# An arena of 29 score slots, divided triples, and an output stage in phases of eight scores

## The chip, the cores and the metric

The kernel runs on one core of a Trainium2 chip, in fp32 throughout (matmuls in fp32 and in the fp32r form). The metric is the device time of one execution in microseconds, the median of the runs shown. Five engines work side by side, each through its own list of instructions in program order: TensorE (PE) multiplies, VectorE (DVE) and ScalarE (ACT) work elementwise, GpSimd (POOL) does small jobs here, and SyncE (SP) issues nearly all DMAs. Semaphores order them against each other. SBUF holds the tiles; PSUM has eight banks that take TensorE's results.

## What is computed

Two blocks read the same x of 2048 rows and 512 columns, and a gate of each row mixes them:

```python
def _A_ref(x, wqkv, wo):
    H = 32; Dh = D // H
    q, k, v = ...                                  # x @ wqkv, 32 heads of 16
    scores = jnp.einsum("bhqd,bhkd->bhqk", q, k) * Dh ** -0.5
    p = _softmax(scores, axis=-1)
    o = jnp.einsum("bhqk,bhkd->bhqd", p, v)
    return o.transpose(0, 2, 1, 3).reshape(B, S, D) @ wo

def _B_ref(x, w1, b1, w2, b2):                     # across the 2048 rows
    h = _layernorm(x, axis=-1)
    u = _gelu(jnp.einsum("bsd,sf->bdf", h, w1) + b1)
    y = jnp.einsum("bdf,fs->bds", u, w2) + b2
    return y.transpose(0, 2, 1)

g = _sigmoid((x * gate_w).sum(-1, keepdims=True))
return g * a + (1 - g) * b
```

The attention has 32 heads of 2048 x 2048 scores. Every score must go through an exponential, and that is most of the work outside TensorE.

## The kernel before

The first 297 us project q, k and v and compute the first layer of block B. From 309 us on attention runs, and beside it two jobs use the half of TensorE's rows that a score leaves free: the second layer of block B, and then the output projection with wo.

**Groups and units.** Two heads and 1024 queries make a group (`NG` = 32 groups). A unit is one score tile: 128 keys by 512 queries of one head, one PSUM bank. A group has 64 units, 32 of each head; the head index `i` picks the row half of TensorE on which the score runs. `RING` = 7 banks are used in turn.

**Phases.** Time is cut into phases. `doubles` lists them in pairs, each entry (size, companions): two phases of `size` scores, in which the same companions run first on the one and then on the other row half. `put(steps, shape, ...)` appends such entries and `call(at, f, ...)` attaches a call to the first phase of entry `at`. Lines 801 to 803 make 92 phases of 12 scores and 30 of 14 for the second layer. Then comes the output stage (46 phases): `open_end` frees the weights and sets up wo, `fetch_tile(t)` and `fetch_o(half, k)` load sums and reciprocals back from DRAM, and `project(t, n)` makes the steps of the output projection of row tile t.

Within a phase the program is written in this order:

1. ScalarE: the exponentials of the scores that were copied in the phase before (`exponential_of_copies`, L1016).
2. TensorE: the scores (`score`, L972), alternating with the companions (L1127). After each, whatever it completes is written: an exponential on ScalarE over one, two or three adjacent banks into as many adjacent slots (`exponential`, L1002), a copy by VectorE out of PSUM (L1121), or, for one unit, an exponential by VectorE itself: a first step out of the bank (L1115) and eight more steps of a polynomial (`steps_of_exp`, L1028 to L1041), spread over the next phases in the list `exp_steps`. `TURN[size]` says which score uses which bank, which of them form single, double or triple exponentials, which are copied, and which banks the V products use.
3. TensorE: the V products (`apply_v`, L926) of the units whose exponentials were written in the phase before, always in pairs of the two query blocks `qb` (`matched`).
4. VectorE: due steps of the list `slow` and of `exp_steps`, as many as fit in `SPAN[size]`, then the sums (`add_sums`, L949).

**The fence.** Companions of the two row halves add into one bank, so they must not overlap: at the last companion of a phase POOL writes `token` (L1133), and the first companion of the next phase waits for it. POOL also clears the sums of a new group (`open_sums`, L862), which waits until the old group in that buffer is stored by SP (`store_sums`, L872, L874).

**Slots.** The exponentials go into `arena`, `SLOTS` = 27 slots of 128 x 512 floats; the last two are scratch of the polynomials (`BOX` = 25), so 25 are handed out. `stamps` holds the free ones with the moment at which they were given back, `take(n)` picks n adjacent free slots and prefers those that were given back before this phase, `give(slot)` returns a slot when its V product has been written. If `exponential` finds no room, or, for the last one of a phase, no three adjacent free slots, it returns False, and the exponential is kept in `put_off` and written behind the phase's V products. There it uses slots which those V products have only just read:

```python
for which in exps:
    if max(which) == m and (put_off or not exponential(units, turn, which, which != exps[-1])):
        put_off.append(which)
```

The fourth argument is `apart`: whether an exponential over several banks may be divided where the slots don't lie together. `wo_hi`, of 8 KB a partition like four slots, has its place beside the arena from the start of attention, and is filled in `open_end`.

**The exponentials on VectorE** start in even phases only and only in the first 18 of a group's 32 units of a head (`DVE_UNTIL`). Sizes 12 and 14 have copies, size 8 has none.

Of the kernel before, what the change touches and what calls it, by code (L numbers as in the profile page):

```python
# [22 lines left out]
P = 128  # L23
S = 2048
D = 512
# [50 lines left out]
def gated_mix(ctx: ExitStack, tc: tile.TileContext, a_x, a_wqkv, a_wo, b_w1, b_b1, b_w2, b_b2, gate_w, out):  # L76
# [495 lines left out]
    BOX = SLOTS - 2  # L572
    SPARE = BOX - 1
    WQ_AT = SPARE - 2
    arena = arena_pool.tile([P, SLOTS, NB], F32, name="arena")
    stamps = {n: 0 for n in range(BOX)}
    room_for = [BOX]
    clock, mark = [0], [0]

    born = {}  # L580
# [1 line left out]
    def take(n, lone=False):  # L582

        room, best = room_for[0], None
        for at in range(room - n + 1):
            slots = range(at, at + n)
            if not all(m in stamps for m in slots):
                continue
            near = [m for b in {m // 3 for m in slots} for m in range(3 * b, min(3 * b + 3, room))]
# [7 lines left out]
            last = max(stamps[m] for m in slots)  # L597
# [12 lines left out]
        stamps[slot] = clock[0]  # L610

    o_parts, o_tile, wo_done = {}, {}, set()
    wo_hi = arena_pool.tile([P, ND, D], F32R, name="wo_hi")
    wo_lo = None

    wq = []

# [33 lines left out]

    def open_end():

        nonlocal end, wo_lo
        u_ctx.close()
        wk_ctx.close()
        end = end_ctx.enter_context(tc.tile_pool(name="end", bufs=1, side="right", reuse_waits="tile"))
        assert all(m in stamps for m in range(SPARE, BOX))
        wo_lo = end.tile([P, ND, D], F32R, name="wo_lo")
        for k in range(ND):  # L660
            raw = base_of(NH + k)
            nc.sync.dma_start(raw, a_wo[k * P : (k + 1) * P, :])
            parts = wo_hi[:, k, :], wo_lo[:, k, :], raw, nc.vector.tensor_copy, nc.vector.tensor_tensor
            whenever(1, 1.1, lambda parts=parts, k=k: (split(*parts), wo_done.add(k)))

        least.append(end.tile([P, 1], F32, name="least"))
# [285 lines left out]
    with tc.manual_schedule(engines=engines):  # L952
# [8 lines left out]
            if done:  # L961
                done()

        at = [0, 0]

        def score(i, bank):

            grp, n = divmod(at[i], GROUP // 2)
            at[i] += 1
            c, qb = n // 2, (n + i) % 2  # L970
            rows = slice(i * HALF, i * HALF + ROWS)
            mm = nc.tensor.matmul(  # L972
                banks[:, bank, :],
                kt[grp][rows, c * P : (c + 1) * P],
                qt[grp][rows, qb * NB : (qb + 1) * NB],
                start=True,
                stop=True,
            )
            writes(mm, bank)
            return Unit(grp, i, c, qb)  # L980

        def hold(unit, slot, when):
            unit.slot, unit.p = slot, arena[:, slot, :]
            waiting[unit.grp].append((when, unit))

        def exponential(units, turn, which, apart=False):
# [4 lines left out]
            while which:  # L991
# [9 lines left out]
                dst = arena[:, slot : slot + n, :]  # L1001
                act = nc.scalar.activation(dst, banks[:, span[0] : span[-1] + 1, :], AF.Exp, scale=SCALE)  # L1002
                reads(act, *span)
                for at, m in enumerate(now):
# [4 lines left out]
        def exponential_of_copies(copied):  # L1009

            while copied:
                slot, n = copied[0][1], 1
                while n < len(copied) and copied[n][1] == slot + n:
                    n += 1
                dst = arena[:, slot : slot + n, :]
                act = nc.scalar.activation(dst, dst, AF.Exp, scale=SCALE)  # L1016
                for unit, at in copied[:n]:
                    unit.source = act
                    hold(unit, at, phase)
                del copied[:n]  # L1020

        def steps_of_exp(unit, slot):

            x = arena[:, slot, :]
            box = [arena[:, BOX + n, :] for n in range(2)]

            def integer():
# [29 lines left out]
        for two, (size, steps) in enumerate(doubles):  # L1057
            for second in range(2):
# [47 lines left out]
                for m, i in enumerate(order):  # L1106
                    units.append(score(i, turn[m]))
                    for which in exps:
                        if max(which) == m and (put_off or not exponential(units, turn, which, which != exps[-1])):
                            put_off.append(which)  # L1110
                    if m in copies:
                        bank = banks[:, turn[m], :]
                        if m in by_dve:
                            slot = take(1, lone=True)
                            ins = nc.vector.tensor_scalar(  # L1115
                                arena[:, slot, :], bank, SCALE * LOG2E, EXP2_LEAST, ALU.mult, ALU.max
                            )
                            exp_steps.extend(steps_of_exp(units[m], slot))
                        else:
                            slot = copies_at[len(copied)]  # L1120
                            ins = nc.vector.tensor_copy(arena[:, slot, :], bank)  # L1121
# [218 lines left out]
```

## Time and profile before

| what | us |
|---|---|
| median of 3 runs | 1596.57 (1595.17 to 1597.18) |
| the profiled execution | 1593.46 |
| its span | 1591.7 |
| TensorE busy | 1371.3 (86%) |
| ScalarE busy | 1088.0 (68%) |
| VectorE busy | 920.2 (58%) |
| GpSimd busy | 203.4 (13%) |
| granted TensorE clock, mean | 0.977 |

In the groups of the page a row gives the source line, engine and operation, the tiles written and read with their shape, the count, the busy time, the mean duration of one in ns, and the idle time of that engine just in front of it with what ended most of it. Matmuls overlap each other, so the mean duration of one is longer than the distance between two. In the chain of work that ended last each step is followed back to what released it. A window's row gives, for a stretch of time, the busy time and count of each engine, the granted clock, the share of the DMA engines and GB/s.

### The profile page before, as it was taken

To read this page: it belongs to the slowest core of one execution; us is meant where nothing else is said; L and a number is where in the kernel's file an instruction comes from. 1 tells how busy PE (TensorE), PEld (TensorE's weight loads), DVE (VectorE), ACT (ScalarE), POOL (GpSimd) and SP (SyncE) were. 2 spreads that over 40 slices of the span, in tenths; PEclk is the share of its full clock that TensorE was granted. 3 is DMA by queue.
4 is the path that set the end of the run, shared out by engine and by line. 5 is a ranking of instruction groups with operands and counts; after the bars stand their busy time and mean duration, and the time that the engine had idled before them with its cause. 6 is when DMAs were issued, how large, how long until landed. Compare 5 with 4: busy or idle time off the path is not lost.

```text
span 1591.7 us, 32727 instructions
## 1 busy us (share of the span) xinstructions
PE 1371.3 (86%) x13274; PEld 828.3 (52%) x13274; DVE 920.2 (58%) x1547; ACT 1088.0 (68%) x1526; POOL 203.4 (13%) x343
## 2 busy tenths in 40 slices
PE   9999999888888988888888888888888777778888
PEld 7888888644444444444444444444444333344445
DVE  5763722766566666565556565465646754555634
ACT  3443433577777887877777788787777766667775
POOL 0211444411010111011010111011010000000000
PEclk9999999899999999999999999999999999999999
DMA  3687332532424233232233233232223343434312
GB/s 126 210 289 252 116 94 82 121 63 52 72 48 76 52 74 58 49 68 57 49 65 61 48 66 61 48 64 59 51 58 76 61 98 82 90 79 97 60 36 78
DMA packets 100175, 133.17 MB, mean 84 GB/s; under 512 B 16729, under 2 KB 63983, under 8 KB 96944
## 3 DMA queue, kind: packets, MB, share of 16 engines
q1 hardware_dynamic: 99440, 129.95, 35.3%
q8 instruction: 106, 1.74, 0.5%
q10 hardware_dynamic: 576, 1.05, 0.2%
q14 instruction: 53, 0.43, 0.1%
HBM read 97.00 MB, written 33.93 MB: 82 GB/s over the span
## 4 chain that ended last, share of the span: by engine, by line
PE 73%; ACT 18%; DMA 3%; issue 2%; DVE 2%; SPq 2%; ACTq 0%; POOL 0%; POOLq 0%; DVEq 0%
PE s L926 27%; PE s L972 24%; ACT arena L1002 17%; PE acc L429 10%; PE acc L90 8%; PE dn L1127 2%; ACT arena L1016 1%; DMA ks<-kp 1%; SPq L515 1%; DMA s<-ot 1%; PE pa L1214 0%; PE acc L201 0%; PE acc L268 0%; DVE ot L949 0%; PE dn L960 0%
## 5 line engine op out<-in xcount | busy, mean ns | idle before, releaser
L1002 ACT ACTIVATE arena<-s 128x512 f32<-128x512 f32 (+2 forms) x1142 | 830.7, 824 | 309.2 <-PE s L926 270.9
L972 PE MATMUL s<-qs,ks 64*128 64x512 f32 x2048 | 581.1, 435 | 183.9 <-ACT arena L1002 165.1
L972 PEld LDWEIGHTS s<-qs,ks 64*128 64x128 f32 x2048 | 338.3, 190 | 430.7 <-ACT arena L1002 320.4
L926 PE MATMUL s<-arena,v 128*17 128x256 f32 x8192 | 487.7, 385 | 16.5 <-ACT arena L1002 16.3
L949 DVE TENSOR_TENSOR ot<-s,ot 128x256 f32<-128x256 f32 (+2 forms) x307 | 153.8, 503 | 345.9 <-PE s L926 312.3
L926 PEld LDWEIGHTS s<-arena,v 128*17 128x17 f32 x8192 | 223.0, 98 | 250.9 <-ACT arena L1002 77.9
L1121 DVE COPY arena<-s 128x512 f32<-128x512 f32 x306 | 207.7, 688 | 102.3 <-PE s L972 92.5
L1127 PE MATMUL dn<-u_hi,w_hi 64*128 64x512 f32 x426 | 181.5, 426 | 0.0
L1127 PE MATMUL dn<-u_lo,w_hi 64*128 64x512 f32 x426 | 178.5, 419 | 0.0
L1127 PE MATMUL dn<-u_hi,w_lo 64*128 64x512 f32 x428 | 177.5, 415 | 0.0
L83 POOL TENSOR_TENSOR w_lo<-w_raw,w_hi 128x512 fp32r<-128x512 f32 (+1 forms) x126 | 155.1, 1232 | 121.2 <-ACT w_hi L82 106.8
L1034 DVE SCALAR_TENSOR_TENSOR arena<-arena 128x512 f32<-128x512 f32 x230 | 163.7, 712 | 6.3
L1016 ACT ACTIVATE arena<-arena 128x1024 f32<-128x1024 f32 (+2 forms) x159 | 163.1, 1027 | 0.0
L1133 POOL MEMSET token<- 1x1 f32 x164 | 15.6, 95 | 840.4 <-PE dn L1127 812.5
L82 ACT CAST w_hi<-w_raw 128x512 fp32r<-128x512 f32 (+1 forms) x67 | 38.1, 569 | 79.9 <-PE acc L429 58.7
L429 PE MATMUL acc<-h_hi,w_hi 128*128 128x512 f32 x224 | 87.1, 389 | 0.0
L429 PE MATMUL acc<-h_lo,w_hi 128*128 128x512 f32 x224 | 87.1, 389 | 0.0
L429 PE MATMUL acc<-h_hi,w_lo 128*128 128x512 f32 x224 | 87.1, 389 | 0.0
L1127 PEld LDWEIGHTS dn<-u_hi,w_lo 64*128 64x128 f32 x428 | 80.2, 187 | 0.6 <-POOL token L1133 0.2
L1127 PEld LDWEIGHTS dn<-u_hi,w_hi 64*128 64x128 f32 x426 | 79.5, 187 | 0.5
L1127 PEld LDWEIGHTS dn<-u_lo,w_hi 64*128 64x128 f32 x426 | 79.4, 186 | 0.5
L1127 PE MATMUL dn<-wo_hi,o_hi 64*128 64x512 f32 x112 | 51.5, 460 | 12.2 <-POOL token L1133 12.2
(144 smaller groups left out, 1245.7 us busy)
## 6 DMA issues: line engine op xcount, KB each, us to landing
w_raw<-in_B_w_dram SPq DMA_DIRECT2D x96, 256.0 KB
ks<-kp SPq DMA_DIRECT2D x192, 128.0 KB
qs<-qp SPq DMA_DIRECT2D x256, 64.0 KB
qp<-pc SPq DMA_DIRECT2D x16, 768.0 KB
x<-in_A_x_dram SPq DMA_DIRECT2D x32, 256.0 KB
kp<-pc SPq DMA_DIRECT2D x16, 512.0 KB
w_raw<-in_B_w_dram SPq DMA_DIRECT2D x32, 128.0 KB
bp<-row SPq DMA_DIRECT2D x16, 256.0 KB
```

The lines of the kernel that those rows point to most:

```text
L82: copy(hi, src)
L83: return sub(lo, src, hi.bitcast(F32), ALU.subtract)
L90: nc.tensor.matmul(ps, a, b, start=start and n == 0, stop=stop and n == last)
L429: nc.tensor.matmul(p, a, b, start=first and k == 0, stop=last and k == 2)
L926: mm = nc.tensor.matmul(av[32 * j : 32 * j + VC, u.i * QC : (u.i + 1) * QC], v[:, u.c, g % NP * 2 + u.i, :], u.p[:, h * QC : (h + 1) * QC] ...
L949: reads(nc.vector.tensor_tensor(x, y, x, ALU.add), bank)
L972: mm = nc.tensor.matmul(banks[:, bank, :], kt[grp][rows, c * P : (c + 1) * P], qt[grp][rows, qb * NB : (qb + 1) * NB], start=True, stop=True,)
L1002: act = nc.scalar.activation(dst, banks[:, span[0] : span[-1] + 1, :], AF.Exp, scale=SCALE)
L1016: act = nc.scalar.activation(dst, dst, AF.Exp, scale=SCALE)
L1034: nc.vector.scalar_tensor_tensor(box[1], box[1] if q is None else q, a, x, ALU.add, ALU.mult)
L1121: ins = nc.vector.tensor_copy(arena[:, slot, :], bank)
L1127: mm = nc.tensor.matmul(ps, a[half], b[half], start=first_of and not second, stop=last_of and bool(second))
```

## The change

The arena gets four more slots, in a tile of their own (`more`, numbered 27 to 30, 29 handed out in all) in the place that `wo_hi` had; `wo_hi` is now made in `open_end`, when `more` is no longer used. `take` works over both. Every exponential may be divided. An exponential of VectorE may start in any phase in which the list of steps is empty, and in phases of eight it takes score 1 away from ScalarE. `score` no longer alternates strictly between the two query blocks but keeps their counts in a group level. The output stage has two phases of 14 without companions and then 62 of 8, where before it had 46 phases of 8, 12 and 14.

```diff
+    MORE = 4
     arena = arena_pool.tile([P, SLOTS, NB], F32, name="arena")
-    stamps = {n: 0 for n in range(BOX)}
-    room_for = [BOX]
+    more_ctx = ExitStack()
+    more_pool = more_ctx.enter_context(tc.tile_pool(name="more", bufs=1, reuse_waits="tile"))
+    more = more_pool.tile([P, MORE, NB], F32, name="more")
+    stamps = {n: 0 for n in (*range(BOX), *range(SLOTS, SLOTS + MORE))}
+    room_for = [SLOTS + MORE]
+
+    def slots(at, n):
+        return arena[:, at : at + n, :] if at < SLOTS else more[:, at - SLOTS : at - SLOTS + n, :]
...
-    wo_hi = arena_pool.tile([P, ND, D], F32R, name="wo_hi")
-    wo_lo = None
+    wo_hi = wo_lo = None
...
         assert all(m in stamps for m in range(SPARE, BOX))
+        assert all(m in stamps for m in range(SLOTS, SLOTS + MORE))
+        more_ctx.close()
+        wo_pool = end_ctx.enter_context(tc.tile_pool(name="wo", bufs=1, reuse_waits="tile"))
+        wo_hi = wo_pool.tile([P, ND, D], F32R, name="wo_hi")
...
-    call(len(doubles) - 4, room, SPARE)
-    call(put([], (8, 0), (12, 0)), open_end)
+    call(len(doubles) - 2, room, SPARE)
+    call(put([], (14, 0), (8, 0)), open_end)
     for t in range(2):
         call(len(doubles) - 2 + t, fetch_tile, t)
     for t in range(NH):
         steps, load = project(t, 3 * ND)
-        at = put(steps, *([(14, 12)] if t % 3 == 2 or t == 7 else [(12, 6), (12, 6)]))
+        at = put(steps, *([(8, 6)] * 2 if t < 2 else [(8, 4)] * 3))
         call(at - 1, load)
         if t + 2 < NH:
             call(len(doubles), fetch_tile, t + 2)
-        if t == 1:
-            call(at, fetch_o, 1, 0)
-        elif t == 4:
-            call(at, fetch_o, 1, 1)
-    call(len(doubles) - 1, fetch_o, 1, 2)
+        if t in (3, 6):
+            call(at, fetch_o, 1, t // 3 - 1)
+    call(len(doubles) - 2, fetch_o, 1, 2)
     for t in range(NH, NS):
         steps, load = project(t, EARLY)
-        call(put(steps, (12 if t < NH + 4 else 8, EARLY)) - 2, load)
+        call(put(steps, (8, EARLY)) - 2, load)
...
-            c, qb = n // 2, (n + i) % 2
+            c = n // 2
+            if n % 2:
+                qb = 1 - began[i]
+            else:
+                more_of = balance.get(grp, 0)
+                qb = began[i] = (n + i) // 2 % 2 if more_of == 0 else int(more_of > 0)
+            balance[grp] = balance.get(grp, 0) + 1 - 2 * qb
...
-                by_dve = copies[:1] if phase % 2 == 0 and at[second] % (GROUP // 2) < DVE_UNTIL else ()
+                by_dve = copies[:1] or (1,) if not exp_steps and at[second] % (GROUP // 2) < DVE_UNTIL else ()
                 for_act = [m for m in copies if m not in by_dve]
+                exps = [which for which in exps if which != by_dve]
...
-                        if max(which) == m and (put_off or not exponential(units, turn, which, which != exps[-1])):
+                        if max(which) == m and (put_off or not exponential(units, turn, which, apart=True)):
                             put_off.append(which)
-                    if m in copies:
+                    if m in copies or m in by_dve:
```

More of the change, by code (lines that the diff above doesn't have):

```diff
@@ L574, in gated_mix, with slot_of @@
     WQ_AT = SPARE - 2
+    MORE = 4
     arena = arena_pool.tile([P, SLOTS, NB], F32, name="arena")
-    stamps = {n: 0 for n in range(BOX)}
-    room_for = [BOX]
+    more_ctx = ExitStack()
[5 more added lines that the diff above has]
+        return arena[:, at : at + n, :] if at < SLOTS else more[:, at - SLOTS : at - SLOTS + n, :]
+    def slot_of(at):
+        return slots(at, 1)[:, 0, :]
     clock, mark = [0], [0]
@@ L585, in take @@
         for at in range(room - n + 1):
-            slots = range(at, at + n)
-            if not all(m in stamps for m in slots):
+            run = range(at, at + n)
+            if not all(m in stamps for m in run):
                 continue
-            near = [m for b in {m // 3 for m in slots} for m in range(3 * b, min(3 * b + 3, room))]
+            near = [m for b in {m // 3 for m in run} for m in range(3 * b, min(3 * b + 3, room)) if m in stamps or m in born]
             others = [born[m] for m in near if m not in stamps]
@@ L596, in take @@
                 fit = 0 if max(others) == phase and not lone else 1 if lone else 3
-            last = max(stamps[m] for m in slots)
+            last = max(stamps[m] for m in run)
             cost = max(last, mark[0]), fit, last, at
@@ L652, in open_end @@
     def open_end():
-        nonlocal end, wo_lo
+        nonlocal end, wo_hi, wo_lo
         u_ctx.close()
@@ L962, in gated_mix @@
                 done()
-        at = [0, 0]
+        at, began, balance = [0, 0], [0, 0], {}
         def score(i, bank):
@@ L982, in hold @@
         def hold(unit, slot, when):
-            unit.slot, unit.p = slot, arena[:, slot, :]
+            unit.slot, unit.p = slot, slot_of(slot)
             waiting[unit.grp].append((when, unit))
@@ L1000, in exponential @@
                 assert span == list(range(span[0], span[0] + n))
-                dst = arena[:, slot : slot + n, :]
+                dst = slots(slot, n)
                 act = nc.scalar.activation(dst, banks[:, span[0] : span[-1] + 1, :], AF.Exp, scale=SCALE)
@@ L1012, in exponential_of_copies @@
                 slot, n = copied[0][1], 1
-                while n < len(copied) and copied[n][1] == slot + n:
+                while n < len(copied) and copied[n][1] == slot + n != SLOTS:
                     n += 1
-                dst = arena[:, slot : slot + n, :]
+                dst = slots(slot, n)
                 act = nc.scalar.activation(dst, dst, AF.Exp, scale=SCALE)
@@ L1022, in steps_of_exp @@
         def steps_of_exp(unit, slot):
-            x = arena[:, slot, :]
+            x = slot_of(slot)
             box = [arena[:, BOX + n, :] for n in range(2)]
@@ L1115, in gated_mix @@
                             ins = nc.vector.tensor_scalar(
-                                arena[:, slot, :], bank, SCALE * LOG2E, EXP2_LEAST, ALU.mult, ALU.max
+                                slot_of(slot), bank, SCALE * LOG2E, EXP2_LEAST, ALU.mult, ALU.max
                             )
@@ L1120, in gated_mix @@
                             slot = copies_at[len(copied)]
-                            ins = nc.vector.tensor_copy(arena[:, slot, :], bank)
+                            ins = nc.vector.tensor_copy(slot_of(slot), bank)
                             copied.append((units[m], slot))
```

## The prediction

> **What bounds the kernel now.** I read the page's chain that ended last and its costliest groups first, then the windows of the two long stretches that the change touches, then the waits inside them, then single phases in the timeline. The page (groups: line, engine, operation, output and input, count, busy us and mean ns, idle time in front and its releaser):
>
> ```profile
> PE 73%; ACT 18%; DMA 3%; issue 2%; DVE 2%; SPq 2%; ACTq 0%; POOL 0%; POOLq 0%; DVEq 0%
> L1002 ACT ACTIVATE arena<-s 128x512 f32<-128x512 f32 (+2 forms) x1142 | 830.7, 824 | 309.2 <-PE s L926 270.9
> L972 PE MATMUL s<-qs,ks 64*128 64x512 f32 x2048 | 581.1, 435 | 183.9 <-ACT arena L1002 165.1
> ```
>
> TensorE and ScalarE alternate on the chain, and each waits for the other: the exponentials (L1002) stand idle 270.9 us for the V products (L926), the scores (L972) 165.1 us for the exponentials. The V products only read arena slots and add into PSUM, so what an exponential can want from them is a slot. The windows (length, then busy us of PE, PEld, DVE, ACT, POOL, clock, DMA share, GB/s), from the first score to the output stage and from there to the last phase's end:
>
> ```profile
> 309.26:1220.32 911.06, 773.47 (x8836) 424.76 (x8837) 553.43 (x929) 708.20 (x964) 94.53 (x204) 0.99 0.32 60
> 1220.32:1572.60 352.28, 282.32 (x2976) 146.23 (x2980) 190.50 (x316) 250.75 (x338) 8.30 (x50) 0.93 0.34 74
> ```
>
> ScalarE is busy for 708.2 of 911.1 us, VectorE for 553.4: neither is full, so the order of waits sets the pace. The waits in the first stretch, and one row of the output stage (total us, times, longest):
>
> ```profile
> ACT arena L1002 <- PE s L926: 191.0, 102, 4.1
> PE s L972 <- ACT arena L1002: 122.3, 111, 3.0
> ...
> ACT arena L1002 <- PE s L926: 79.9, 39, 5.1
> ```
>
> One such wait in the timeline (start, duration, instruction, idle in front and releaser):
>
> ```profile
> 610.03 3.22 PE L926 MATMUL s<-arena,v 128*17 128x256 f32 x56
> 613.37 1.45 ACT L1002 ACTIVATE arena<-s 128x1536 f32<-128x1536 f32 x1 [1.99 <-PE s L926]
> 614.88 0.50 PE L972 MATMUL s<-qs,ks 64*128 64x512 f32 x1 [1.63 <-ACT arena L1002]
> 616.10 4.00 ACT L1002 ACTIVATE arena<-s 128x512 f32<-128x512 f32 x8
> ```
>
> The last exponential of a phase covers three banks and found no three adjacent free slots. It is put behind the phase's V products, so ScalarE idles 1.99 us, then TensorE 1.63 us for the bank. Following take() and give() through the code, 103 of the 122 phases before the output stage put a triple off, against 102 waits counted above; in the output stage 36 of 46 do, against 39.
>
> **The change, part by part.**
>
> *Four more slots, divided triples (first stretch).* By the same following, the changed kernel puts a triple off in 2 of the 122 phases and 2 of the 64 of the output stage. Arithmetic hardly moves: copies and polynomials on VectorE stay at 238 and 36 in this stretch, and ScalarE's exponentials go from 1301 to 1246 in the whole program. The phases stay too: lines 801 to 803 make 92 of 12 scores and 30 of 14. So the question is what a phase takes without a late triple. The trace has some:
>
> ```profile
> 651.46 0.50 PE L972 MATMUL s<-qs,ks 64*128 64x512 f32 x1
> 652.15 4.80 ACT L1002 ACTIVATE arena<-s 128x512 f32<-128x512 f32 x6
> 654.32 2.79 PE L926 MATMUL s<-arena,v 128*17 128x256 f32 x48
> 656.73 1.17 ACT L1016 ACTIVATE arena<-arena 128x1024 f32<-128x1024 f32 x1
> 657.67 0.71 ACT L1002 ACTIVATE arena<-s 128x512 f32<-128x512 f32 x1
> ...
> 651.46:663.10 11.64, 10.92 (x138) 6.25 (x134) 4.71 (x9) 11.64 (x15) 1.47 (x3) 1.00 0.28 69
> ...
> 593.50 0.50 PE L972 MATMUL s<-qs,ks 64*128 64x512 f32 x1
> 599.79 0.50 PE L972 MATMUL s<-qs,ks 64*128 64x512 f32 x1
> ```
>
> From 651.46 two such 12-score phases take 11.64 us, 5.82 each, with ScalarE busy throughout: four singles and two triples from 652.15 to 656.73 (4.58 us), the two copied scores 0.94, together 5.52. TensorE needs 2.86 us for 12 scores (651.46 to 654.32) and 2.79 for 48 V products, 5.65. The two engines nearly balance. A pair of V products is 8 rows of the trace, 2.79/6 = 0.465 us; phases with 7 or 8 pairs (3.3 and 3.7 us) are longer on TensorE, those with 5 shorter; a phase between a punctual and a late one, 593.50 to 599.79, took 6.29 with 7 pairs. Between 5.82 and 6.29 I take 6.1. For 14 scores TensorE needs 2.86 x 14/12 + 3.22 = 6.6, ScalarE 5.52 plus one single (0.50, eight in 4.00 us) plus a third copy (0.47) = 6.5; the other end is 6.29 x 14/12 = 7.3; I take 7.0. Sum 92 x 6.1 + 30 x 7.0 = 771 us: **140 us gained**. The ends: 92 x 5.82 + 30 x 6.6 = 733 (gain 178), and 92 x 6.29 + 30 x 7.3 = 798 (gain 113). ScalarE's 708.2 busy us are a floor below both. Cover for VectorE: its 553.4 us would fill 72% of 771. `more` lies where wo_hi lay and is emptied before the output stage, so it costs nothing itself; a divided triple adds at most 2 x 0.50 + 0.50 - 1.45, under 0.1 us.
>
> *Output stage in phases of eight.* It goes from 46 phases to 64 for the same 524 scores: two of 14 without companions, then 62 of 8. The end of the kernel now already runs five like them:
>
> ```profile
> 1549.11:1568.65 19.54, 19.54 (x244) 11.45 (x240) 9.21 (x17) 19.17 (x26) 0.44 (x5) 1.00 0.19 58
> ```
>
> 19.54/5 = 3.91 us each, TensorE full, eight companions. The last 16 new phases are the same. The other 46 have 0 to 6 companions, so scores pair up in the two row halves and TensorE drops below; ScalarE then holds them at two singles and three doubles, 2 x 0.50 + 3 x 0.94 = 3.8. That makes 46 x 3.8 + 16 x 3.91 = 237 us. The two phases of 14 put their triples off: V products 3.22, two triples 2 x 1.45, scores 3.3, about 9.3 each, 18.5.
>
> What gets worse is slack. A closed group stores its sums; POOL clears the buffer only after that store and writes the next fence token behind it, and the first companion of the phase after that waits for the token:
>
> ```profile
> 588.40 0.50 PE L972 MATMUL s<-qs,ks 64*128 64x512 f32 x1
> 593.27 0.53 POOL L862 MEMSET ot<- 128x512 f32 x1 [7.83 <-DMA s<-ot]
> 593.73 0.09 POOL L1133 MEMSET token<- 1x1 f32 x1
> 593.87 0.49 PE L1127 MATMUL dn<-u_hi,w_lo 64*128 64x512 f32 x1
> ...
> 1292.97 6.44 DMA s<-ot
> 1300.33 0.79 PE L1127 MATMUL dn<-wo_hi,o_hi 64*128 64x512 f32 x1 [6.09 <-POOL token L1133]
> 1300.00:1304.00 4.00, 3.67 (x17) 2.80 (x17) 3.64 (x7) 1.48 (x3) 0.36 (x3) 0.52 0.00 0
> ```
>
> At 588.40 the token came 5.3 us into the phase that follows the closing one, so in phases near 6 us the fence stays covered. In phases of 3.8 us it is 1.7 us late, for 8 groups. Where key and query loads (14 DMAs) and a tile's 8 fetches stand ahead of the store on SP, the store lands late and costs what 1293 shows: 6.09 us, and 4 us at clock 0.52 behind it, another 2. Ends: 8 x 1.7 = 14 and 8 x 8.1 = 65; two of the eight have fetches ahead of them, so I take 8 x 4 = 32. The fetches have the same problem on VectorE, whose quotients stay due one phase after the fetch:
>
> ```profile
> 1246.94 0.69 DVE L698 TENSOR_TENSOR arena<-o_lo,o_hi 128x512 f32<-128x512 f32 x1 [4.46 <-DMA row<-bp]
> ```
>
> A phase shorter by 3.5 us exposes more of it; sums (L949) and the bank behind them wait. 16 quotients at 0 to 4.46 us is 0 to 71; VectorE has slack of most of a phase, so I take 14. The 15 polynomials (10 now) and 5 copies (68 now) lighten VectorE: nothing on the path. Sum: 18.5 + 237 + 32 + 14 = 302 against 352.3: **50 us gained**, ends 270 and 397.
>
> [...]
>
> *Sum.* The profiled execution took 1593.46 us, span 1591.7. Less 140 and 50 it is 1403; the median of the runs is 3.1 above the profiled one, so **1406 us**.
>
> **The rivals.**
>
> *Nearly all of the idle time comes back.* ScalarE's steady rhythm of 5.52 us would hold, fences would hide. For it: 11.64 of 11.64 busy at 651.46. Against it: V products come in uneven lots, 5 to 8 pairs. Time: 733 and 270, 1593.5 - 178 - 82 + 3 = 1336.
>
> *The wait only moves.* Punctual triples leave the banks to VectorE's copies and sums, queued behind polynomial steps of 0.7 us, and the output stage is eaten up by fences and quotients. For it: VectorE at 72%, and an end of 397. Against it: 4.71 busy us in 11.64 above. Time: first stretch 798 or a little more, output stage 365, two thirds of the way from 302 to 397: 1593.5 - 113 + 13 + 3 = 1497.
>
> *The four slots don't do it*, because triples still find none: 4 late phases of 186 are left, so only a mistake in the following would give this: the output stage alone, 1593.5 - 50 + 3 = 1547.
>
> *Slower: the half clock settles in.* If the waits of the output stage return so often that TensorE stays near the 0.52 of 1300 us, a phase of eight takes 3.7/0.52 = 7.1 us. 62 x 7.1 + 18.5 + 46 = 505 against 352.3 loses 153, and eats the 140: 1610. It decides from 6.9 us a phase. For it: the stage's clock is 0.93 now, with waits of 6 us. Against it: 1.00 from 1549 to 1568 with phases of eight.
>
> **How the numbers follow.** Forecast 0.62 (its own range 1370 to 1450), idle time back 0.16, moved wait 0.16, no effect 0.01, half clock 0.05. The range 1335 to 1500 reaches the times of both neighbours and leaves out what lies beyond them, the half clock too: under 2 in 10. This kernel's measurement can tell about 0.2% (3 us) from no change: faster 0.94, same 0.01, slower 0.05, the last for the half clock.
>
> **What would show it.** Right: ScalarE's idle time for L926 in the first stretch falls from 191 us to under 40 and the stretch to about 771 us, with ScalarE over 88% busy; phases of eight come every 3.8 us, with up to eight waits of POOL's token on TensorE and a few of L698 on DMA. Wrong: TensorE waits for L1121 or L949 instead, or the output stage stays above 340 us.

## The result, and the profile after

| | before | after |
|---|---|---|
| median, us | 1596.36 (1595.17 to 1597.18, 4 runs) | 1437.21 (1433.17 to 1440.22, 4 runs) |
| the profiled execution | 1593.46 | 1433.17 |
| its span | 1591.7 | 1431.3 |
| first score | 309.26 | 304.29 |
| first stretch (first score to output stage) | 911.06 | 778.18 |
| output stage | 352.28 | 329.93 |
| granted clock, mean | 0.977 | 0.965 |

The ratio is 0.9002, with an interval of 0.8975 to 0.9029. Of the 160.3 us between the two profiled executions, 132.9 come from the first stretch, 22.4 from the output stage and 5.0 from an earlier first score.

In the code of after, the exponentials are L1020 (they were L1002), the scores L990 (L972), the V products L938 (L926), the companions L1146 (L1127), the token L1152 (L1133), the clearing of the sums L874 (L862), the sums L961 (L949), the quotients L712 (L698). The chain that ended last and the costliest groups, from the page of after:

```profile
PE 65%; DMA 11%; ACT 8%; DVE 7%; SPq 6%; issue 3%; POOL 0%; POOLq 0%; DVEq 0%; ACTq 0%
...
L1020 ACT ACTIVATE arena<-s 128x512 f32<-128x512 f32 (+2 forms) x1029 | 778.5, 873 | 148.1 <-PE s L990 116.7
L990 PE MATMUL s<-qs,ks 64*128 64x512 f32 x2048 | 531.4, 424 | 42.7 <-DVE ot L961 22.3
```

ScalarE's exponentials no longer stand idle for the V products; what they still wait for is the next score. The scores' idle time fell from 183.9 to 42.7 us. ScalarE's share of the chain fell from 18% to 8%, and DMA and the DMA issue on SP, 5% together before, are now 17%, which points to the next limit. The windows of the two stretches:

```profile
304.29:1082.47 778.18, 731.83 (x8836) 422.39 (x8836) 529.05 (x925) 706.86 (x934) 93.56 (x206) 0.99 0.38 71
1082.47:1412.40 329.93, 270.27 (x2976) 145.23 (x2980) 182.86 (x315) 244.38 (x313) 10.00 (x68) 0.88 0.35 78
```

ScalarE has as much to do as before (706.9 us), in 778.2 us: 91% busy. In the output stage TensorE is busy for 270.3 of 329.9 us at a clock of 0.88, so time is lost there. Some of the waits of the first stretch (total us, times, longest; "..." marks rows left out):

```profile
ACT arena L1020 <- PE s L990: 48.8, 60, 4.2
...
PE dn L1146 <- POOL token L1152: 13.8, 12, 2.8
...
PE s L990 <- DVE ot L961: 12.4, 19, 1.3
...
ACT arena L1020 <- PE s L938: 8.2, 2, 4.8
```

And of the output stage:

```profile
PE dn L1146 <- POOL token L1152: 42.4, 6, 9.7
...
DVE arena L712 <- DMA o<-ot: 18.5, 2, 9.8
...
PE s L990 <- DVE ot L961: 9.9, 8, 5.2
DVE arena L712 <- DMA o_hi<-r: 9.5, 6, 4.0
```

The 191.0 us in 102 waits of the first stretch are down to 8.2 us in 2, the two late triples that are left there. TensorE now waits for POOL's token, 12 times in the first stretch and 6 times in the output stage. A piece of the steady rhythm in the timeline of ScalarE:

```profile
602.43 1.09 ACT L1034 ACTIVATE more<-more 128x1024 f32<-128x1024 f32 x1
603.38 4.79 ACT L1020 ACTIVATE arena<-s 128x512 f32<-128x512 f32 x6
607.99 1.11 ACT L1034 ACTIVATE arena<-arena 128x1024 f32<-128x1024 f32 x1
609.25 2.59 ACT L1020 ACTIVATE arena<-s 128x512 f32<-128x512 f32 x5 [0.16 <-PE dn L1146]
```

Where 1.99 us of idle time stood ahead of the triple at 613.37 before, nothing over 0.16 us is left in this piece.

Of the 61 phases of eight whose length can be read from score to score, 52 take 3.80 us on average. The other nine take 7.0 to 15.5 us, and six of them come two phases after a group has closed. Here is one of these, in the timelines of SP (the queue), POOL and TensorE; the phase begins at 1345.89, the one before it at 1342.42:

```profile
1337.24 4.93 SPq L515 DMA_DIRECT2D qs<-qp  x8
1342.21 2.74 SPq L515 DMA_DIRECT2D ks<-kp  x6
1345.00 0.42 SPq L763 DMA_DIRECT2D base<-bp  x1
1345.52 2.32 SPq L884 DMA_DIRECT2D o<-ot  x4
1348.61 0.56 SPq L886 DMA_DIRECT2D s<-ot  x1
...
1340.76 0.09 POOL L1152 MEMSET token<- 1x1 f32 x1 [4.57 <-PE dn L1146]
1353.12 0.53 POOL L874 MEMSET ot<- 128x512 f32 x1 [12.27 <-DMA s<-ot]
1353.58 0.09 POOL L1152 MEMSET token<- 1x1 f32 x1
...
1353.72 0.79 PE L1146 MATMUL dn<-wo_hi,o_hi 64*128 64x512 f32 x1 [7.33 <-POOL token L1152]
```

The next loads of a group (14 DMAs, L515) hold SP from 1337.24 to 1344.95. Only then can the closed group's sums be stored (L884, L886), which ends on the queue at 1349.17; the buffer is cleared when the store has landed, 3.95 us later; the token stands behind the clearing on POOL; and TensorE's queue stands 7.33 us for it.

### The profile page after: what moved, and what is told of

Read it like the earlier page. It is cut to its first block, busy times and chain, and to the rows that moved or that the text cites. A ratio compares the mean times of both kernels' runs of the same rounds, so it can differ in the third digit from the quotient of the medians.

```text
span 1431.3 us, 32692 instructions
## 1 busy us (share of the span) xinstructions
PE 1317.0 (92%) x13274; PEld 824.5 (58%) x13274; DVE 885.2 (62%) x1541; ACT 1080.0 (75%) x1471; POOL 203.2 (14%) x361
## 4 chain that ended last, share of the span: by engine, by line
PE 65%; DMA 11%; ACT 8%; DVE 7%; SPq 6%; issue 3%; POOL 0%; POOLq 0%; DVEq 0%; ACTq 0%
PE s L938 22%; PE s L990 17%; PE acc L429 10%; PE acc L90 9%; ACT arena L1020 6%; PE dn L1146 5%; SPq L515 4%; DMA ks<-kp 3%; DMA o<-ot 3%; DVE ot L961 2%; DMA s<-ot 2%; DVE arena L1052 2%; SPq L884 1%; DMA o_hi<-r 1%; ACT more L1020 1%
## 5 line engine op out<-in xcount | busy, mean ns | idle before, releaser
L1020 ACT ACTIVATE arena<-s 128x512 f32<-128x512 f32 (+2 forms) x1029 | 778.5, 873 | 148.1 <-PE s L990 116.7
L990 PE MATMUL s<-qs,ks 64*128 64x512 f32 x2048 | 531.4, 424 | 42.7 <-DVE ot L961 22.3
L938 PE MATMUL s<-arena,v 128*17 128x256 f32 x7372 | 480.2, 388 | 5.9 <-ACT arena L1020 4.8
L990 PEld LDWEIGHTS s<-qs,ks 64*128 64x128 f32 x2048 | 337.9, 190 | 223.7 <-ACT arena L1020 58.9
L938 PEld LDWEIGHTS s<-arena,v 128*17 128x17 f32 x7372 | 211.9, 99 | 220.3 <-ACT arena L1020 52.3
L961 DVE TENSOR_TENSOR ot<-s,ot 128x256 f32<-128x256 f32 (+2 forms) x314 | 150.4, 500 | 301.1 <-PE s L938 255.6
L1146 PE MATMUL dn<-u_hi,w_hi 64*128 64x512 f32 x426 | 177.3, 416 | 4.2 <-POOL token L1152 4.2
L1146 PE MATMUL dn<-u_hi,w_lo 64*128 64x512 f32 x428 | 174.0, 407 | 5.4 <-POOL token L1152 5.4
L1146 PE MATMUL dn<-u_lo,w_hi 64*128 64x512 f32 x426 | 174.7, 410 | 4.3 <-POOL token L1152 4.3
L1140 DVE COPY arena<-s 128x512 f32<-128x512 f32 x201 | 130.6, 682 | 12.9 <-PE s L990 12.3
L1152 POOL MEMSET token<- 1x1 f32 x182 | 16.7, 92 | 674.3 <-PE dn L1146 610.1
L1034 ACT ACTIVATE arena<-arena 128x1024 f32<-128x1024 f32 (+2 forms) x100 | 112.1, 1121 | 0.0
L82 ACT CAST w_hi<-w_raw 128x512 fp32r<-128x512 f32 (+1 forms) x67 | 38.1, 569 | 79.7 <-PE acc L429 58.7
L938 PE MATMUL s<-more,v 128*17 128x256 f32 x820 | 92.6, 382 | 1.6 <-ACT arena L1020 1.6
L1020 ACT ACTIVATE more<-s 128x512 f32<-128x512 f32 (+2 forms) x93 | 84.9, 947 | 8.9 <-PE s L990 8.8
L1146 PEld LDWEIGHTS dn<-u_hi,w_lo 64*128 64x128 f32 x428 | 80.0, 187 | 9.5 <-POOL token L1152 7.0
L1146 PEld LDWEIGHTS dn<-u_lo,w_hi 64*128 64x128 f32 x426 | 79.4, 186 | 7.9 <-POOL token L1152 5.9
```

The costliest lines, as they stand in the source:

```text
L938: mm = nc.tensor.matmul(av[32 * j : 32 * j + VC, u.i * QC : (u.i + 1) * QC], v[:, u.c, g % NP * 2 + u.i, :], u.p[:, h * QC : (h + 1) * QC] ...
L961: reads(nc.vector.tensor_tensor(x, y, x, ALU.add), bank)
L990: mm = nc.tensor.matmul(banks[:, bank, :], kt[grp][rows, c * P : (c + 1) * P], qt[grp][rows, qb * NB : (qb + 1) * NB], start=True, stop=True,)
L1140: ins = nc.vector.tensor_copy(slot_of(slot), bank)
L1146: mm = nc.tensor.matmul(ps, a[half], b[half], start=first_of and not second, stop=last_of and bool(second))
```

## The experiments

Three theories stood at the start. The late triples set the pace of the first stretch, whichever part of the change removes them. In the output stage the clearing ahead of the token holds TensorE; its rival is that the quotients, which wait for their fetches, hold VectorE's sums and so the banks. Stretches below are from the first score to the output stage, and from there to the last phase's end.

| run | median, us | ratio to before | phases with a late triple, first stretch | first stretch | output stage |
|---|---|---|---|---|---|
| before | 1596.36 | | 103 | 911.1 | 352.3 |
| after | 1437.21 | 0.9002 | 2 | 778.2 | 329.9 |
| e1_clear_later | 1400.64 | 0.8771 [0.8753, 0.8790] | 2 | 764.9 | 310.4 |
| e2_quotients_later | 1424.74 | 0.8933 [0.8912, 0.8954] | 2 | 775.7 | 320.6 |
| e3_both_later | 1381.61 | 0.8651 [0.8636, 0.8666] | 2 | 765.1 | 290.1 |
| e4_old_output | 1456.27 | 0.9116 [0.9096, 0.9136] | 4 | 778.8 | 350.4 |
| e5_eights_only | 1574.73 | 0.9866 [0.9844, 0.9887] | 105 | 918.8 | 325.7 |
| e6_no_division | 1485.35 | 0.9302 [0.9285, 0.9318] | 42 | 826.2 | 332.2 |
| e7_more2 | 1484.90 | 0.9302 [0.9284, 0.9320] | 42 | 826.8 | 330.1 |
| e10_loads_after | 1397.41 | 0.8751 [0.8735, 0.8768] | 2 | 765.0 | 307.4 |
| e12_loads_between | 1377.11 | 0.8631 [0.8610, 0.8652] | 2 | 764.3 | 288.8 |
| e13_old_turns_and_rule | 1433.88 | 0.8997 [0.8973, 0.9020] | 2 | 780.3 | 325.5 |
| e14_halves_later | 1358.70 | 0.8523 [0.8509, 0.8538] | 2 | 764.8 | 268.0 |

The phases with a late triple are followed through take() and give() in the code, as in the prediction.

**Two halves of the change alone.** e4 is after with before's list of phases in the output stage:

```diff
-        at = put(steps, *([(8, 6)] * 2 if t < 2 else [(8, 4)] * 3))
+        at = put(steps, *([(14, 12)] if t % 3 == 2 or t == 7 else [(12, 6), (12, 6)]))
...
-        call(put(steps, (8, EARLY)) - 2, load)
+        call(put(steps, (12 if t < NH + 4 else 8, EARLY)) - 2, load)
```

> Slots, division, turns of the query blocks and VectorE's rule as changed, but the output stage in the phases of 12, 14 and 8 of before. Theory S (the first stretch's gain is that of the slots alone, and the phases of eight bring only the output stage's own): first stretch 775 to 785 us as in the changed kernel, output stage 335 to 350 with 27 late triples, median 1440 to 1460. Rival T (the phases of eight are worth nothing, their extra fences eat them): output stage 325 to 332, median 1432 to 1440.

e5 is the reverse: before, with after's list of phases in the output stage and nothing else.

> The kernel before with the output stage in phases of eight and nothing else. Theory S: first stretch 905 to 915 us as before, output stage 325 to 340 (352 before, 330 in the changed kernel), median 1570 to 1585. Rival (phases of eight need the extra slots or VectorE's share): output stage 345 or more, 1590 to 1600.

e4 has the whole gain of the first stretch and an output stage like before's (350.4 against 352.3), though the triples put off there fell from 36 to 27. e5 has the output stage's gain and a first stretch 7.7 us longer than before's. Alone they gain 140.1 and 21.6 us, 161.7 together, against 159.2 for both: within the spread of the runs the two halves are independent.

**Other numbers of late triples.** In e6 the last exponential of a phase may not be divided, as in before; the four slots stay:

```diff
-                        if max(which) == m and (put_off or not exponential(units, turn, which, apart=True)):
+                        if max(which) == m and (put_off or not exponential(units, turn, which, which != exps[-1])):
```

> As changed, but the last exponential of a phase is again put off where no three adjacent slots are free: 42 late triples in the first stretch instead of 2 (103 in the kernel before). Theory S: the first stretch grows by 1.3 us for each late triple (133 us for 101 of them between the two kernels), 778 + 52 = 830 us, median 1480 to 1495. Rival: the slots alone bring it, a late triple that finds slots free since the phase before costs nothing, median 1437 to 1450.

In e7 triples may be divided, but there are two more slots instead of four:

```diff
-    MORE = 4
+    MORE = 2
```

> As changed, but two more slots instead of four: 42 late triples in the first stretch, as many as without division, but others, and 32 more exponentials. Theory S (the number of late triples sets the time): 1478 to 1492, as without division (1485). Rival (the number of slots sets it): half of the way between 25 and 29 slots, about 1510.

Both leave 42 late triples, by different means, and both come out at the same first stretch, 826.2 and 826.8 us. The waits of ScalarE in the first stretch of e6:

```profile
ACT arena L1020 <- PE s L938: 87.9, 39, 3.6
ACT arena L1020 <- PE s L990: 24.0, 32, 4.1
ACT more L1020 <- PE s L938: 6.6, 3, 2.5
```

39 and 3 waits stand for 42 late triples. From 42 to 2 the stretch loses 826.2 - 778.2 = 48 us, 1.2 each, and from 103 to 42 it loses 84.9, 1.4 each. TensorE's waits for the token, none in before, 5.6 us in e6 and 13.8 in after, hide a part: without them it is 1.4 and 1.5 us each. So the number of late triples sets the first stretch, whether it comes down by room or by division. (e7 has 54 more exponentials there than e6, not the 32 of the expectation: 828 against 774 in the groups of their profiles up to 1140 us. The time doesn't show them.)

**The other two edits.** e13 takes back the turns of the query blocks and VectorE's rule, so that VectorE computes no exponentials in the output stage:

```diff
-                qb = began[i] = (n + i) // 2 % 2 if more_of == 0 else int(more_of > 0)
+                qb = began[i] = (n + i) % 2
...
-                by_dve = copies[:1] or (1,) if not exp_steps and at[second] % (GROUP // 2) < DVE_UNTIL else ()
+                by_dve = copies[:1] if phase % 2 == 0 and at[second] % (GROUP // 2) < DVE_UNTIL else ()
```

> As changed, but the query blocks alternate as before and VectorE's exponentials start in even phases and with a copy only, so there are none in phases of eight (15 in the changed kernel). Theory S (only slots, division and the output stage's phases count): within 8 us of the changed kernel, 1429 to 1446. Rival (VectorE's share carries the phases of eight): output stage 10 us or more longer, 1447 or more.

1433.88 us, from 1431.61 to 1436.89, overlaps after's 1433.17 to 1440.22. These two edits gain nothing that shows. The medians of the five runs so far all lie in the ranges of their first theories.

**The clearing behind the fence.** e1 writes the clearing three phases later, when the store has had time to land, so that POOL's tokens come first:

```diff
-                        open_sums(grp + 2)
+                        if grp + 2 < NG:
+                            later(3, open_sums, grp + 2)
```

> The sums of a new group are cleared three phases after the old group is stored, so POOL's fence token no longer stands behind that store. Theory A (the fence is what holds the output stage at 330 us instead of 302): the six waits of TensorE for the token, 42.4 us in the output stage, and the half clock behind them go, as do some 14 us of short ones in the first stretch: output stage 270 to 290 us, median 1370 to 1390. Rival B (quotients on VectorE that wait for their fetches hold the same phases): token waits go, but the long phases stay, median 1417 to 1435.

It gained 36.6 us, less than the first theory expected and more than the rival. No wait for the token is left in either stretch. The first stretch gained 13.3 us, as much as its token waits were (13.8). But of the 42.4 us of the output stage only 19.5 came back. The waits of VectorE for fetches grew there from 28.0 to 38.1 us, those of TensorE's scores for the sums (L961) from 9.9 to 37.8, and VectorE's timeline shows one of the phases that stayed long:

```profile
1136.93 0.69 DVE L712 TENSOR_TENSOR arena<-o_lo,o_hi 128x512 f32<-128x512 f32 x1 [10.54 <-DMA o<-ot]
1137.66 0.43 DVE L82 CAST o_hi<-arena 128x512 fp32r<-128x512 f32 x1
1138.12 0.69 DVE L83 TENSOR_TENSOR o_lo<-arena,o_hi 128x512 fp32r<-128x512 f32 x1
1138.73 1.41 DVE L1052 SCALAR_TENSOR_TENSOR arena<-arena 128x512 f32<-128x512 f32 x2
1140.06 0.41 DVE L961 TENSOR_TENSOR ot<-s,ot 128x256 f32<-128x256 f32 x1
```

The quotient waits 10.54 us for its fetch (the row names the group's store, which is later on the same queue; the quotient reads only `o_lo` and `o_hi`, which the fetch fills), and the sums (L961), which free a bank for the next score, stand behind it on VectorE. Of the six phases that had waited for the token, four fell to their normal length. The two in which a tile's fetches share SP with the group's loads stayed, at 16.4 and 15.4 us: there both waits had stood side by side. Two more places are held by quotients alone, 18.3 us in two neighbouring phases and 11.2 us in another.

**The quotients.** e2 leaves the clearing as it is and makes the quotients due two phases after their fetch:

```diff
-            whenever(2 if n < P // DH else 1, 1.75, lambda i=i: divide(i))
+            whenever(2 if n < P // DH else 2, 1.75, lambda i=i: divide(i))
...
-        whenever(1, 1.75, divide)
+        whenever(2, 1.75, divide)
```

> The quotients are due two phases after their fetch instead of one; the fence is as in the changed kernel. Theory A: VectorE's waits for the fetches, about 28 us in total, shrink, but the fence holds the same phases, 1425 to 1437. Rival B: the output stage loses 20 to 35 us, 1402 to 1417.

12.5 us were gained, at the edge of the first expectation and short of the rival. The six token waits of the output stage stayed (41.3 us). e3 has both edits:

> Sums cleared three phases later and quotients due two phases after their fetch, both together. Alone they brought 37 and 12 us; clearing later left the phases 132, 148 and 160 at 16.4, 15.4 and 11.2 us, in which the sums wait behind a quotient that waits for its fetch. Theory A+B (fence and quotient hold the same phases, one behind the other): together more than the sum, those three phases fall to 5 to 9 us, median 1370 to 1390. Rival (what holds them is SP, whose fetches stand behind 14 loads of keys and queries): they stay at 11 to 15 us, 1388 to 1400.

55.6 us were gained, more than 36.6 and 12.5 together (49.1): in two phases each wait had covered the other. The median is in the range of the first theory, but besides the first phase of eight (8.2 us) three stayed long, 10.4, 13.4 and 7.7 us, which leans to the rival. The chain in the profile of e3, at the longest of them (start, length, what):

```profile
1159.90 0.42 SPq L515
...
1163.88 5.24 DMA row<-bp
...
1173.19 0.69 SPq L720
...
1173.93 8.74 DMA o_hi<-r
```

The 14 loads, a store and eight fetches of a tile go through SP one after the other, and the reciprocals issued behind them (`o_hi` from `r`) take 8.74 us to land, so the quotient is late even with two phases' notice.

**The loads of a group.** If the loads are what the rest stands behind, they should go elsewhere. e10 is e3 with all loads in the output stage one phase later (`later(1, load_group, done_to + 1)`).

> Both delays, and in the output stage the loads of a group's keys and queries are issued one phase later, behind that phase's fetches and stores. Theory (SP's order is the last thing that holds phases of eight): no phase over 8 us behind phase 124, output stage 255 to 275, median 1355 to 1375. Rival (the DMA engines are busy with the same bytes in the same few phases either way): no better than both delays alone within 5 us.

It lost 15.8 us against e3, which neither theory had: the loads now came ahead of other fetches, and besides the first phase of eight four long ones took 12.8, 19.2, 15.1 and 10.0 us. e12 is e3 with only those loads moved that meet fetches, each to where SP is free:

```diff
+    OUT, LOAD_LATER = len(doubles), {123: 2, 130: 1, 138: 3, 146: 1}
...
+                        if two >= OUT and phase in LOAD_LATER:
+                            later(LOAD_LATER[phase], load_group, done_to + 1)
+                        else:
+                            load_group(done_to + 1)
```

> Both delays, and the loads of keys and queries of four groups of the output stage moved to phases in which no fetch comes behind them (from 123 to 125, 130 to 131, 138 to 141, 146 to 147). The run with all loads one phase later was 16 us slower than both delays alone, since the loads then stood ahead of the fetches of 124 and 140. Theory (the order on SP decides: a fetch must not stand behind 14 loads): phases 133, 143 and 149 fall from 10.4, 13.4 and 7.7 to 4 to 6, median 1360 to 1372. Rival (the DMA engines' load decides): 1377 to 1390.

It gained 4.5 us against e3, and 1377.11 is the lower edge of the rival's range. The phases at 133 and 149 were cured, but one at 127 now took 14.4 us; the chain of e12 there:

```profile
1105.90 0.42 SPq L515
...
1106.82 0.42 SPq L515
...
1107.29 6.07 DMA rc<-s
```

The loads moved from phase 123 had come ahead of the small load that VectorE's reciprocals wait for. And the phase at 143 stayed, at 11.0 us: there the large fetch took 9.40 us to land, though no loads stood ahead of it, only a store and a tile's eight fetches. e14 leaves the loads of phase 123 where they were and makes the quotients of the first two large fetches (`fetch_o`) due four phases after them:

```diff
-    OUT, LOAD_LATER = len(doubles), {123: 2, 130: 1, 138: 3, 146: 1}
+    OUT, LOAD_LATER = len(doubles), {130: 1, 138: 3, 146: 1}
...
-            whenever(2 if n < P // DH else 2, 1.75, lambda i=i: divide(i))
+            whenever(4 if k < 2 else 2, 1.75, lambda i=i: divide(i))
```

> Both delays; the group loads of 130, 138 and 146 (not of 123) stand behind the fetches; the quotients of the two large fetches with time to spare are due four phases after them instead of two. In the run before this one the phase 127 took 14.4 us behind a small load that stood behind the moved loads of 123, and 143 took 11.0 us behind a large fetch that itself took 9.4 us to land. Theory (each long phase is VectorE behind one late transfer, and goes when that transfer gets time): 127 and 143 fall to 4 to 5 us, median 1358 to 1368. Rival (the bytes of the stage are the limit, the wait turns up at the next phase): 1374 to 1382.

1358.70 us: 78.5 us (5.5%) less than after, and a ratio of 0.8523 to before. The windows of e14:

```profile
304.29:1069.07 764.78, 730.62 (x8836) 418.48 (x8836) 539.83 (x925) 706.07 (x934) 100.19 (x206) 0.99 0.38 72
1069.07:1337.06 267.99, 254.71 (x2976) 137.42 (x2980) 182.98 (x315) 242.41 (x315) 10.75 (x68) 0.97 0.43 96
```

TensorE is busy for 95% of the output stage at a clock of 0.97 (82% and 0.88 in after). Of the phases of eight only two still take over 5 us (8.2, the first of them, and 5.7). What stayed is the seam of the two stretches: four phases of 14 around it take 9.8, 10.5, 12.5 and 10.6 us, with the late triples that are left and a mean granted clock of 0.84 (over the four of after, from 1061.04 to 1105.33, it is 0.81). No run tried to mend that.

## Why the prediction came out as it did

The forecast of 1406 us was 31 us below the median, inside the stated range. The sum was 771 + 302; measured were 778.2 + 329.9. Point by point:

**The first stretch was sized rightly: 771 against 778.2 us.** Phases of 12 were put at 6.1 and took 6.12; phases of 14 at 7.0 and took 7.18. The signs came too: 8.2 us of waits for the V products (under 40 was asked), ScalarE 91% busy (over 88%). That it came within 7 us is luck in part: the second phase and the last two, priced like all others, took 36.7 us instead of 20.1, and the other 119 phases took 741 us where 751 were counted, of which 14 are the token waits below. Why the second phase takes 12.8 us stays open. That late triples are the cause is shown by e6 and e7, where 42 of them cost about 48 us whichever edit leaves them.

**"In phases near 6 us the fence stays covered" failed, by a small sum.** The token of 593.73 came 5.3 us into a phase that was itself 5.1 us long, and the next companion, at 593.87, took it at once: no cover was left there. Phases of 12 scores took 7.0 us on average in before; at 6.1 us twelve waits of up to 2.8 us came up, 13.8 us, and e1, which removes them, brings the stretch to 764.9: the prediction's 771 stands between the stretch with them and without.

**"46 x 3.8 + 16 x 3.91" was right for undisturbed phases:** 52 phases took 3.80 us on average. The two phases of 14 took 12.3 and 10.5 us, 22.9 together, where 18.5 were counted (the three parts given for one add up to 9.4 us, not 9.3).

**The step that failed is the price of the stalls: 32 us for fences and 14 for quotients, 46.** The 62 phases took 307.1 us, 71 more than 62 x 3.80. The six phases with a token wait carry 57 us of it, 9.5 each, where 4 for each of eight was taken; the three others carry 15. (Of the eight closings, one comes just ahead of phases without companions, and one has no later group to clear for.) The prediction had taken the token as coming 5.3 us into the phase after the closing one, as it did at 588.40, which put the companion 1.7 us late in a phase of 3.8; only where fetches stood ahead was a long wait supposed, for two of eight. But the lag isn't a constant. In the phase shown above the token came 1353.58 - 1342.42 = 11.2 us into that phase, with no fetch ahead: the loads ended 2.5 us into it, the store with the row ahead of it took until 6.8, landing another 4.0. In before the 14 loads at that place had left SP at 585.4, 3.0 us before the phase of 588.40 began: the closing phase, 7.3 us long, was enough for them. Shorter phases brought the loads and the store together: ahead of all six waits SP's queue shows the store right behind the 14 loads, or behind them and a tile's eight fetches. So all six became long ones, of 4.8 to 9.7 us, 7.1 on average. Of the two ends given for the fences, 14 and 65, the upper one was nearly met. (The upper end of the whole stage adds up to 18.5 + 237 + 65 + 71 = 392 us, not 397.)

**The quotients were sized about right, but not as a sum of their own.** Waits of 28.0 us for fetches stood on VectorE in after, 18.5 of them in two phases that waited for the token at the same time. e1 made them visible: removing 42.4 us of token waits gave 19.5 there. The sum counted fences and quotients side by side; where two waits stand in the same phase, the longer one is paid, and removing one alone shows the other.

**The half clock.** The windows of after with the wait of 7.33 us, and the 3.5 us and then 10 us behind it:

```profile
1346.00:1353.70 7.70, 0.39 (x1) 0.07 (x1) 2.63 (x5) 1.28 (x2) 0.55 (x2) 0.71 0.91 198
1353.70:1357.20 3.50, 3.48 (x15) 2.46 (x15) 0.00 (x0) 2.32 (x3) 0.00 (x0) 0.50 0.16 59
1357.20:1367.20 10.00, 10.00 (x117) 5.41 (x120) 6.01 (x12) 6.67 (x10) 0.26 (x3) 0.89 0.01 2
```

TensorE ran at 0.50 for 3.5 us, and 0.89 over the next 10 stands for another 10 x 0.11/0.5 = 2.2 us at half: 5.7 us at half speed, of which about half, 2.8 us, came on top of the wait, where the prediction added 2. (At 0.50 one score follows the other after 0.43 us, at 1.00 after 0.23.) Ahead of that, 0.71 over 7.70 us is half speed for 4.5 of them. Narrower windows show the same: 1.00 from 1346.40 to 1349.20, 0.50 from 1349.50 to 1359.00, 0.57 in the next half microsecond, and 1.00 from 1359.50 on. So here the clock fell 2.8 us after TensorE stopped at 1346.4, and was full again 5.7 us after it went on at 1353.72. Behind the waits of 9.68 and 5.72 us, which ended at 1150.85 and 1188.41, it was full again after 3.8 us each. At the first phase of eight the clock fell without a wait of that length (TensorE's timeline, then two windows):

```profile
1103.88 0.63 PE L938 MATMUL s<-arena,v 128*17 128x256 f32 x8 [1.64 <-ACT arena L1020]
1105.33 0.73 PE L990 MATMUL s<-qs,ks 64*128 64x512 f32 x3 [0.81 <-DVE ot L961]
...
1108.30 5.32 PE L938 MATMUL s<-arena,v 128*17 128x256 f32 x48
...
1100.02:1106.84 6.82, 4.21 (x56) 1.59 (x47) 3.51 (x8) 3.65 (x3) 0.00 (x0) 1.00 0.03 9
...
1106.84:1113.67 6.83, 6.20 (x53) 2.26 (x51) 2.10 (x4) 3.91 (x6) 0.53 (x1) 0.50 0.31 86
```

No wait in the first window is longer than 1.64 us; TensorE was busy for 4.21 of its 6.82 us. Behind it the clock was 0.50 for 6.83 us: 48 V products took 5.32 us, where as many took 2.79 in before at 654.32, at a clock of 1.00. No run shows what made the clock fall there. The 4.4 us that this phase takes over 3.80, a part of the 15 above, are neither fence nor quotient; in every run with the new list of phases it took 7.0 to 8.2 us.

The half clock did not settle in, as that rival would have it: an average phase of eight took 4.97 us, the turning point was 6.9, and with the waits gone (e14) the stage is at 0.97.

**The other rivals.** "Nearly all of the idle time comes back" would need 733 us; even without token waits the stretch stays at 765. "The wait only moves" to VectorE asked for waits for copies and sums in the first stretch. TensorE's matmuls for scores wait there 12.4 us for sums and 4.0 for copies (3.3 and 3.2 in before), a small part of what was removed; in the output stage its mechanism is real, at 330 instead of 365 us. "The four slots don't do it" fell with e4.

**What the sum didn't have.** The first score came 5.0 us earlier; see the last section.

## What to carry to other kernels

When an engine idles behind work that only frees its buffers, count the late cases by following the allocator: the stretch here went with that number, at 1.2 to 1.4 us each, whether room or division brought it down. What is short can also be room that lies together: e6 keeps all 29 slots and 42 of the 103 late triples.

When phases get shorter, every lag that is counted in phases must be worked out anew in microseconds: the way from a group's loads and store to the token was covered in phases of 7 us, cost up to 2.8 us in phases of 6, and 4.8 to 9.7 us in phases of 3.8, where the loads held the queue for 7.7. Look then at what else sits on the same queue, and take away all the waits of one phase together; e1 and e2 alone gave 49 us, both together 56, and with the loads sorted 78.

## What the runs showed of the hardware that was not expected

**With other places in SBUF the first score came earlier.** SP's queue at the start of attention, in before:

```profile
294.47 2.73 SPq L515 DMA_DIRECT2D ks<-kp  x6
305.40 3.56 SPq L515 DMA_DIRECT2D qs<-qp  x8
```

and in after:

```profile
294.15 2.88 SPq L515 DMA_DIRECT2D ks<-kp  x6
297.07 5.94 SPq L515 DMA_DIRECT2D qs<-qp  x8
```

The query loads stood 8 us behind the key loads in before and come right after them now. All runs with `wo_hi` out of the arena's pool have their first score at 304.3 to 306.6, and e5, with the old places, at 309.3. What the query loads waited for stands in SP's waits, from 285 to 331 us, in before:

```profile
SPq L515 <- DVE u_lo L451: 8.1, 1, 8.1
```

L451 is VectorE's last step of the first layer of block B. The same row has 7.7 us in e5, 0.4 in after and 0.5 in e14. That the wait comes from an earlier tile in the same place is argued, since of the whole change only the moved tiles bear on the work ahead of the first score; it wasn't tried by itself.

**The landing of a DMA behind others.** In e3 the reciprocals took 8.74 us from issue to landing behind the loads, a store and a tile's eight fetches, and in e12 a small load took 6.07 us behind 14 loads. But the large fetch of e12 at 143 took 9.40 us with no loads ahead of it and 14 right behind. Where the loads stand matters: moving them by one phase each cost 15.8 us (e10), by chosen numbers of phases it was a part of what gained 22.9 (e14, both against e3). The runs do not separate the order on the queue from the bytes that move in the same few us.
